# Re-set planner constants, array modes told apart and a lag behind a bank's copy, in a two-layer attention and MoE kernel on one core

## The chip, the core and the metric

The kernel runs on one core of a Trainium2 chip. The metric is device time in microseconds (us) for one execution, from the first to the last instruction with what lies around them; lower is better. The kernel before takes 907.85 us, the median of three runs (905.75 to 908.74).

## What is computed

Three stages follow each other. Attention has 4 batches, 8 heads, 576 tokens and 64 features per head; it is linear attention with random features:

```python
def phi(x):
    proj = np.einsum('bhsd,md->bhsm', x, omega)          # 128 features
    h = proj - np.sum(x * x, axis=-1, keepdims=True) / 2.0
    return np.exp(h - np.max(h, axis=-1, keepdims=True)) / np.sqrt(m)
num = phi(q) @ (phi(k).T @ v);  den = phi(q) @ sum_s phi(k) + 1e-06
x = (num / den)                                          # 2304 tokens x 512
x = leaky(x @ w_in) @ w_out                              # layer one, d_ff 2048
x = (h * clip(h + 3, 0, 6) / 6) @ w2_out,  h = x @ w2_in # layer two, d_ff 2048
```

All inputs are float32. The products of the two layers keep float32 accuracy by splitting every operand in a high and a low part of type fp32r and adding three matmuls (high by high, low by high, high by low).

## The kernel before

The 2304 tokens are cut into five groups (512, 256, 512, 512, 512). Layer one (`moe1`) takes the groups in turn: for each of 16 blocks of 128 hidden features it runs 12 matmuls of the first product (`Hblk`, by `mm3`, lines L478 to L480), an activation, a split into parts `g`, and 12 matmuls of the second product (`Oblk`). Attention of a later group (`K_unit`, `Q_unit`) is mixed between these products. Attention of the first group (`Q_first`) runs alone at the start, since nothing else is ready there.

TensorE's array is used in three ways. The layers' products and the transposes use all of it. The scores of attention (`scores` and `K_tail`, L721 and L742) use two halves of 64 rows; two products of attention (L790 in `K_unit`, L949 in `Q_unit`) use two halves of 64 columns.

Layer two (`moe2`) has a Strassen-like scheme for the groups of 512 tokens: seven products of half size in place of eight, both in the first product (`Hpair`, 7 products of 6 matmuls with 256 columns each, L1122) and in the second (`down`, 7 products of 3 matmuls, L1044). In `Hpair` four of the seven products (b11, t2, t3, t4) are accumulated one after another in the same half of one bank, R[0]. After b11, t2 and t3 ScalarE or VectorE copies this half to SBUF (`save`, a copy through the helper at L463 and L464), and the next product may write the half only when the copy is done; after t4 it is copied once more. The four adds between the quarters that `down` needs (`parts`, through `plus` and `add_alts`, L471 on VectorE, L472 on GpSimd) and the split in high and low parts (`halves`) run between `Hpair` and `down`.

No order is written by hand. Every step is an `Op` in a `Graph`: its alternatives (engine, cost in ns, function), a due time, the buffers that it takes and the steps that it depends on. `Graph.run` repeats one thing: among the steps whose inputs are planned, it takes the one that can start first by its own clocks (within 60 ns the one due first), picks the engine that ends it first (with a `BIAS` against VectorE, 300 ns in the last phase) and emits it. So each engine's order is fixed when the program is built. A step of attention on TensorE also waits in the plan for `SLACK` (2000 ns) after it is ready, or for `FOLLOW` (400 ns) if the step before it on TensorE was one of attention too, and a change between the two kinds is planned with `SWITCH` (110 ns). In the first stage planned gaps of TensorE are half filled with matmuls on zeros (`keep_warm`, L1317), 15 of them ahead of everything. Due times of layer two come from `UP` and `DOWN` (ns for one pair of blocks), `LAG_A` (how many pairs `down` stays behind), `READY`, `XLEAD` and `SOON`.

## Time and profile before

| what | value |
|---|---|
| median of three runs | 907.85 us (905.75 to 908.74) |
| the profiled execution | 907.79 us, of which the span from first to last instruction 906.0 us |
| TensorE busy (PE) | 892.0 us, 98% of the span |
| weight loads busy (PEld) | 796.2 us, 88% |
| VectorE (DVE), ScalarE (ACT), GpSimd (POOL) | 617.0, 492.8, 332.0 us |
| granted TensorE clock | 1.0 in all but the first and last instants |
| HBM traffic | 217 GB/s over the span |

The profile is one execution on the core. PE is TensorE's matmuls, PEld its weight loads, which run beside them. The end of a matmul is modelled (two follow each other much faster than one seems to last), so the pace of TensorE is read from start to start, or from how many matmuls lie in a stretch, and not from its busy share. By time there are three stages: attention of the first group alone (to about 49 us), layer one with the rest of attention (to about 536 us), and layer two.

### The profile page before, as it was taken

Reading aid. Unit: us, or ns where it says so; the run is one execution under the profiler, and the core shown is the slowest. Engines: PE = TensorE matmul, PEld = TensorE weight load, DVE = VectorE, ACT = ScalarE, POOL = GpSimd, SP = SyncE. Lnnn points to the kernel's source line nnn. Section 1 sums busy time; section 2 is a strip of 40 time slices with the busy share of each in tenths; the row PEclk is TensorE's granted clock in tenths of the full one; section 3 lists DMA queues with packets and bytes.
Section 4 is the critical chain, followed back from the end, with each engine's and each line's share of the span. In section 5 each row is a group of like instructions: output and inputs, shape, how many; then the busy total and the mean of one; then the engine's idle time right before and its main releaser. Section 6 shows DMA issues by size and latency. Waiting matters only on the chain.

```text
span 906.0 us, 17804 instructions
## 1 busy us (share of the span) xinstructions
PE 892.0 (98%) x6349; PEld 796.2 (88%) x6349; DVE 617.0 (68%) x1464; ACT 492.8 (54%) x1155; POOL 332.0 (37%) x559
## 2 busy tenths in 40 slices
PE   8999999999999999999999999999999999999998
PEld 8878888889777877888888888999999999999997
DVE  5998877877897976555687344675665658666554
ACT  6966674866776555544455345543443444445442
POOL 3454454544535321101010003244426436454642
PEclk9999999999999999999999999999999999999999
DMA  9556644677557555978899349885786684677540
GB/s 333 152 167 215 204 153 139 208 228 232 149 171 223 178 166 178 367 286 314 292 343 349 95 140 326 280 296 168 244 311 218 201 260 131 224 242 231 167 134 28
DMA packets 91497, 198.01 MB, mean 219 GB/s; under 512 B 14736, under 2 KB 40976, under 8 KB 91408
## 3 DMA queue, kind: packets, MB, share of 16 engines
q1 hardware_dynamic: 91408, 196.87, 65.7%
q8 instruction: 50, 0.82, 0.4%
q14 instruction: 39, 0.32, 0.1%
HBM read 150.18 MB, written 46.66 MB: 217 GB/s over the span
## 4 chain that ended last, share of the span: by engine, by line
PE 91%; DVE 4%; ACT 2%; issue 1%; DMA 1%; POOL 1%; SPq 0%; DVEq 0%; POOLq 0%; ACTq 0%
PE bank L1044 18%; PE bank L1122 17%; PE bank L478 15%; PE bank L480 15%; PE bank L479 15%; PE bank L721 4%; PE bank L768 1%; PE bank L949 1%; PE bank L918 1%; PE bank L790 1%; DVE junk L892 1%; PE bank L844 1%; DMA late_w<-in 1%; DVE nm L686 1%; PE bank L779 0%
## 5 line engine op out<-in xcount | busy, mean ns | idle before, releaser
L1044 PE MATMUL bank<-w,g 128*128 128x256 f32 x762 | 108.1, 279 | 0.4 <-DVE g L467 0.2
L1044 PEld LDWEIGHTS bank<-w,g 128*128 128x128 f32 x762 | 96.9, 188 | 1.0 <-DVE g L467 0.7
L464 ACT COPY late_u<-bank 128x256 f32<-128x256 f32 (+1 forms) x112 | 43.1, 386 | 95.1 <-PE bank L1122 86.4
L986 DVE TENSOR_TENSOR g<-bank,g 128x512 fp32r<-128x512 f32 (+1 forms) x80 | 50.8, 635 | 60.9 <-ACT g L464 60.2
L984 ACT ACTIVATE bank<-bank 128x512 f32<-128x512 f32 (+1 forms) x80 | 43.8, 548 | 76.2 <-PE bank L480 76.0
L1122 PE MATMUL bank<-x,late_w 128*128 128x256 f32 x552 | 74.0, 281 | 0.9 <-DVE u L1065 0.7
L697 ACT ACTIVATE h<-bank,nm 128x128 f32<-128x128 f32 x228 | 63.5, 390 | 18.9 <-POOL nm L692 18.7
L1122 PEld LDWEIGHTS bank<-x,late_w 128*128 128x128 f32 x552 | 68.2, 189 | 1.5 <-DVE u L1065 0.9
L1122 PE MATMUL bank<-second_w,late_w 128*128 128x256 f32 x498 | 68.5, 281 | 0.5 <-ACT late_u L464 0.5
L478 PE MATMUL bank<-g,w 128*128 128x512 f32 (+1 forms) x180 | 68.9, 383 | 0.0
L478 PE MATMUL bank<-x,w 128*128 128x512 f32 (+1 forms) x180 | 68.7, 382 | 0.1
L480 PE MATMUL bank<-g,w 128*128 128x512 f32 (+1 forms) x180 | 66.3, 368 | 0.8 <-DVE g L986 0.8
L480 PE MATMUL bank<-x,w 128*128 128x512 f32 (+1 forms) x180 | 66.4, 369 | 0.5 <-POOL x L468 0.5
L479 PE MATMUL bank<-g,w 128*128 128x512 f32 (+1 forms) x180 | 66.2, 368 | 0.0
L479 PE MATMUL bank<-x,w 128*128 128x512 f32 (+1 forms) x180 | 66.2, 368 | 0.0
L1122 PEld LDWEIGHTS bank<-second_w,late_w 128*128 128x128 f32 x498 | 62.4, 189 | 0.8 <-ACT late_u L464 0.7
L686 DVE TENSOR_REDUCE nm<-bank 128x4 f32<-128x512 f32 (+2 forms) x76 | 48.1, 654 | 15.8 <-PE bank L721 15.7
L1044 PE MATMUL bank<-second_w,g 128*128 128x256 f32 x333 | 48.8, 280 | 0.0
L903 POOL TENSOR_TENSOR h<-h,den 128x512 f32<-128x512 f32 (+2 forms) x32 | 33.1, 1038 | 41.8 <-DVE den L898 25.4
L692 POOL TENSOR_TENSOR nm<-nm,sq 128x4 f32<-128x4 f32 (+2 forms) x76 | 25.2, 344 | 60.2 <-DVE nm L689 57.2
L478 PE MATMUL bank<-x,second_w 128*128 128x512 f32 (+1 forms) x120 | 45.2, 377 | 0.3 <-ACT h L697 0.3
L472 POOL TENSOR_TENSOR xr<-late_xr 128x128 f32<-128x128 f32 x38 | 19.3, 526 | 70.7 <-DVE late_xr L1160 70.7
(361 smaller groups left out, 2449.9 us busy)
## 6 DMA issues: line engine op xcount, KB each, us to landing
late_w<-in SPq DMA_DIRECT2D x84, 512.0 KB, 4.5
in<-late_w SPq DMA_DIRECT2D x32, 512.0 KB, 3.8
late_w<-in SPq DMA_DIRECT2D x40, 256.0 KB, 4.5
third_w<-in SPq DMA_DIRECT2D x20, 512.0 KB, 4.4
wst<-w2i SPq DMA_DIRECT2D x16, 512.0 KB, 4.2
wst<-w2o SPq DMA_DIRECT2D x16, 512.0 KB, 4.1
x_t<-late_w SPq DMA_DIRECT2D x12, 512.0 KB, 4.5
wst<-w1i SPq DMA_DIRECT2D x10, 512.0 KB, 4.6
```

The lines of the kernel that those rows point to most:

```text
L464: return [("act", c_act(n, psum), lambda: nc.scalar.copy(dst(), src())), dve if psum else dve + (True,)]
L478: nc.tensor.matmul(o, lhsT=ah, rhs=bh, start=start, stop=False)
L479: nc.tensor.matmul(o, lhsT=al, rhs=bh, start=False, stop=False)
L480: nc.tensor.matmul(o, lhsT=ah, rhs=bl, start=False, stop=stop)
L686: g.op([("dve", c_dve(c * 128), lambda raw=raw, n_=n_: nc.vector.tensor_reduce(out=n_()[:, :, 0], in_=raw(), axis=AX.X, op=ALU.min))], rd= ...
L697: nc.scalar.activation(h.tiles[0][:, q * 128:q * 128 + 128], raw()[:, q], AF.Exp, bias=nm.tiles[0][:, q], scale=-1.0)
L721: nc.tensor.matmul(ps[bank].tiles[0][o, at:at + 128], lhsT=src.tiles[0][r, k * one + i * 128:k * one + i * 128 + n], rhs=wn[r], start=True ...
L903: eng.tensor_tensor(out=x, in0=x, in1=den.tiles[1][:, 0:c].to_broadcast([128, c, 128]), op=ALU.mult)
L984: g.op([("act", c_act(n, True), lambda: nc.scalar.activation(P(), P(), AF.Prelu, alpha=0.01))], wr=[p], due=d)
L986: g.op([("dve", c_dve(n), lambda: nc.vector.tensor_tensor(out=G1(), in0=P(), in1=G0().bitcast(F32), op=ALU.subtract))], rd=[p, (gg, 0)], w ...
L1044: nc.tensor.matmul(acc[bank].tiles[0][:, half * 256:half * 256 + 256], lhsT=src.tiles[x][:, q * 128:q * 128 + 128], rhs=w[k].tiles[y][:, c ...
L1122: nc.tensor.matmul(R[r](), lhsT=w[x], rhs=m[y], start=start and k == n == 0, stop=k == 1 and n == 2, skip_group_check=True)
```

## The change

The planner now tells modes of the array apart. Each attention step on TensorE has a mode: S (halves of rows), N (halves of columns) or F (the whole array); products of the layers are M. How long a step waits in the plan after it is ready depends on its mode and on that of the step before it; a turn from one mode to another has a planned cost of its own. In layer two a product into R[0] that accumulates on a half copied before (t2, t3, t4) is planned at least `APART` = 100 ns after it is ready, so that another ready step may go first. `LAT`, costs, caps on live buffers, due times and lags are re-set, the first stage gets a fourth buffer `xT`, and `BIAS2`, the planner's bias against VectorE in the last phase, falls from 300 to 200 ns. What is computed, the number of matmuls of the computation and their shapes stay as they are.

```diff
-SLACK = 2000.0
-FOLLOW, SWITCH = 400.0, 110.0
+SLACK = 1.0
+PACE = 2.215
+WAIT = {"S": 4000.0, "N": 1000.0, "F": 1500.0}
+FOLLOW = 400.0
+MATE = 400.0
+TURN = {("M", "S"): 193.0, ("M", "N"): 92.0, ("S", "M"): 205.0, ("N", "M"): 158.0, ("F", "S"): 193.0, ...
-NW1 = 10
+NW1 = 11
-BIAS2 = 300.0
+BIAS2 = 200.0
-ATT = [None, (32e3, 132e3), (132e3, 182e3), (182e3, 240e3), (240e3, 300e3)]
+ATT = [None, (32000.0, 132000.0), (132e3, 178000.0), (182e3, 236000.0), (240e3, 305000.0)]
-UP, DOWN = 7.2e3, 2.5e3
+UP, DOWN = 7100.0, 2600.0
+APART = 100.0
-LAG_A, XLEAD, SOON, READY = 3.0, 9e3, 10e3, 14e3
+LAG_A, XLEAD, SOON, READY = 2.5, 6000.0, 13000.0, 15000.0
...
-    LAT = 150.0
+    LAT = 165.0
-    CAP = {"x2": 5, "s": 2, "h": 4, "sum": 4, "raw": 6}
+    CAP = {"x2": 6, "s": 1, "h": 6, "sum": 4, "raw": 6}
...
-        last = False
+        last = "M"
...
-                at = o.ready + (FOLLOW if o.slack and last else o.slack) + o.lazy
+                at = o.ready + (self.wait(o.mode, last) if o.slack else 0.0) + o.lazy
...
-                if last != (o.slack > 0.0):
-                    clock["pe"] += SWITCH
-                    o.end += SWITCH
-                last = o.slack > 0.0
+                turn_ = TURN.get((last, o.mode), 0.0)
+                clock["pe"] += turn_
+                o.end += turn_
+                last = o.mode
...
+    @staticmethod
+    def wait(mode, last):
+        if mode == "F":
+            return FOLLOW if last != "M" else WAIT["F"]
+        return MATE if last in "SN" else FOLLOW if last == "F" else WAIT[mode]
...
-    first, more = room("first", [("h", 6, ([128, 512], F32)), ("xT", 3, ([128, 512], F32)), ("xn", 2, ([128, 8, D], F32)),
+    first, more = room("first", [("h", 6, ([128, 512], F32)), ("xT", 4, ([128, 512], F32)), ("xn", 2, ([128, 8, D], F32)),
...
-                g.op([("pe", 6 * c_mm(256), mm)], rd=[c[a], b], wr=[bank[r]], due=t0 + UP * at)
+                g.op([("pe", 6 * c_mm(256), mm)], rd=[c[a], b], wr=[bank[r]], due=t0 + UP * at, lag=APART if r == 0 and not start else 0.0)
```

What this does to the program shows in the order of the instructions. The lines named here are 13 higher in the changed kernel (L1122 becomes L1135, L1044 becomes L1057, L472 becomes L485); a row is one instruction, with the number of equal ones behind an x.

**TensorE in layer two**, the seventh pair of blocks of the third group, from t2 to t4. R[0] is in bank_177 before and in bank_178 in the changed kernel; rows of L1044 and L1057 are products of `down`. Before:

```order
L1122 MATMUL bank_177<-second_w_4_0_1024,third_w_0_0_1595 128x256 x6
L1044 MATMUL bank_176<-w_95,g_105 128x256 x3
L1044 MATMUL bank_180<-w_94,g_105 128x256 x3
L1122 MATMUL bank_177<-second_w_3_0_1023,late_w_2_0_3977 128x256 x6
L1044 MATMUL bank_179<-w_96,g_105 128x256 x3
L1044 MATMUL bank_175<-w_97,g_106 128x256 x3
L1122 MATMUL bank_177<-x_101,late_w_3_0_3978 128x256 x6
```

Now:

```order
L1135 MATMUL bank_178<-w_92,late_w_0_0_3974 128x256 x6
L1057 MATMUL bank_182<-second_w_0_0_1054,g_106 128x256 x3
L1057 MATMUL bank_176<-w_98,g_105 128x256 x3
L1057 MATMUL bank_181<-w_98,g_105 128x256 x3
L1057 MATMUL bank_176<-second_w_0_0_1054,g_105 128x256 x3
L1057 MATMUL bank_183<-w_99,g_105 128x256 x3
L1135 MATMUL bank_178<-second_w_3_0_1057,late_w_2_0_3976 128x256 x6
L1135 MATMUL bank_177<-x_103,late_w_3_0_3977 128x256 x6
L1135 MATMUL bank_180<-x_104,late_w_3_0_3977 128x256 x6
L1135 MATMUL bank_178<-x_101,third_w_0_0_1613 128x256 x6
```

Between one product into R[0] and the next there were 6 matmuls; now there are 15 and 12, partly of `down` and partly of the next pair.

**TensorE in the first stage**, from the second gap that is filled with matmuls on zeros. Before (the rows that follow are the product L768 of attention, which needs the features of the first K unit):

```order
L1317 MATMUL bank_182<-zero 128x384 x12
L768 MATMUL bank_180<-first_v_0_0_169,ht_0_152 128x132
L768 MATMUL bank_180<-first_v_0_0_169,first_h_0_0_158 128x66
L768 MATMUL bank_180<-first_v_0_0_169,first_h_1_0_159 128x66
L768 MATMUL bank_180<-first_v_0_0_169,first_h_0_0_158 128x66
```

Now (L734 is the scores, from the fourth buffer `first_xT_3`):

```order
L1330 MATMUL bank_183<-zero 128x384 x5
L734 MATMUL bank_181<-wn,first_xT_3_0_167 128x128
L734 MATMUL bank_182<-wn,first_xT_3_0_167 128x128
L734 MATMUL bank_181<-wn,first_xT_3_0_167 128x128
L734 MATMUL bank_182<-wn,first_xT_3_0_167 128x128
L734 MATMUL bank_181<-wn,first_xT_3_0_167 128x128
L734 MATMUL bank_182<-wn,first_xT_3_0_167 128x128
L734 MATMUL bank_181<-wn,first_xT_3_0_167 128x128
L734 MATMUL bank_182<-wn,first_xT_3_0_167 128x128
L1330 MATMUL bank_183<-zero 128x384 x4
L781 MATMUL bank_176<-first_v_0_0_170,ht_0_152 128x132
```

The scores of a third unit moved into the gap; in the whole stage 45 matmuls on zeros became 34.

**The adds of `parts`**, at the end of the third group of layer two. Before, on GpSimd, the four adds each for two sets of quarters (one set in xr_0_115, one in xr_0_112):

```order
L468 TENSOR_TENSOR second_w_1_0_1021<-xr_0_113,second_w_1_0_1021 128x512
L472 TENSOR_TENSOR xr_0_115<-late_xr_1_0_3986 128x128 x2
L472 TENSOR_TENSOR xr_0_115<-xr_0_115,late_xr_1_0_3986 128x128
L472 TENSOR_TENSOR xr_0_112<-wst_0_108 128x128
L472 TENSOR_TENSOR xr_0_115<-late_xr_1_0_3986,xr_0_115 128x128
L472 TENSOR_TENSOR xr_0_112<-xr_0_112,wst_0_108 128x128
L472 TENSOR_TENSOR xr_0_112<-wst_0_108 128x128
L472 TENSOR_TENSOR xr_0_112<-wst_0_108,xr_0_112 128x128
```

Now, on VectorE, behind its work on the last pair of the group:

```order
L1173 SCALAR_TENSOR_TENSOR late_xr_1_0_3985<-bank_180,late_u_0_0_3979 128x2x128
L1173 SCALAR_TENSOR_TENSOR wt_0_111<-bank_180,late_u_0_0_3979 128x2x128
L480 TENSOR_TENSOR g_105<-xr_0_114,g_105 128x512
L480 TENSOR_TENSOR g_107<-late_xr_1_0_3985,g_107 128x384
L484 TENSOR_TENSOR xr_0_113<-xr_0_113,late_xr_1_0_3985 128x128
L484 TENSOR_TENSOR xr_0_113<-late_xr_1_0_3985 128x128
L484 TENSOR_TENSOR xr_0_113<-late_xr_1_0_3985,xr_0_113 128x128
L484 TENSOR_TENSOR xr_0_112<-xr_0_112,wst_0_108 128x128
```

In the whole program 170 adds of 128 columns moved from GpSimd (288 before, 118 now) to VectorE (none before).

## Rows read from the trace of the kernel before

**Rows 1.** Windows: length, busy us (count) of PE, PEld, DVE, ACT, POOL, clock, DMA, GB/s.

```profile
0.00:49.30 49.30, 45.08 (x405) 41.09 (x405) 37.05 (x95) 39.51 (x113) 19.78 (x46) 1.00 0.73 248
49.30:536.00 486.70, 483.59 (x2874) 394.80 (x2873) 357.95 (x881) 287.90 (x705) 149.60 (x206) 1.00 0.65 217
536.00:560.50 24.50, 23.25 (x169) 21.32 (x168) 9.73 (x23) 11.45 (x24) 5.89 (x12) 1.00 0.86 295
560.50:760.00 199.50, 199.50 (x1712) 199.50 (x1711) 124.94 (x285) 91.98 (x188) 89.43 (x169) 1.00 0.74 245
769.00:868.50 99.50, 99.50 (x850) 99.50 (x849) 59.86 (x131) 45.58 (x96) 47.53 (x95) 1.00 0.67 210
```

**Rows 2.** Waits of PE in layer two (536 to 902 us): us, times, longest.

```profile
PE bank L1122 <- ACT late_u L464: 0.8, 3, 0.5
```

**Rows 3.** A window inside layer two, columns as in rows 1.

```profile
592.00:621.00 29.00, 29.00 (x259) 29.00 (x258) 18.39 (x41) 11.14 (x22) 14.28 (x29) 1.00 0.73 256
```

**Rows 4.** Timeline of PE from 703.9 us: start, length, what, count [idle before].

```profile
703.91 1.58 PE L1122 MATMUL bank<-x,late_w 128*128 128x256 f32 x12
705.33 1.58 PE L1044 MATMUL bank<-second_w,g 128*128 128x256 f32 x12
...
768.64 0.62 PE L1122 MATMUL bank<-x,late_w 128*128 128x256 f32 x3 [0.70 <-DVE u L1065]
```

**Rows 5.** Timeline of PE from 620.5 us: t3, the next product, t4.

```profile
620.54 0.84 PE L1122 MATMUL bank<-second_w,late_w 128*128 128x256 f32 x6
621.22 0.84 PE L1122 MATMUL bank<-x,late_w 128*128 128x256 f32 x6
621.90 0.92 PE L1122 MATMUL bank<-x,third_w 128*128 128x256 f32 x6
622.65 0.52 PE L1044 MATMUL bank<-w,g 128*128 128x256 f32 x3
```

**Rows 6.** Timeline of ACT, same place: the copy of R[0] after t3.

```profile
621.42 0.37 ACT L464 COPY late_u<-bank 128x256 f32<-128x256 f32 x1 [1.98 <-PE bank L1122]
```

**Rows 7.** Timeline of PEld, same place: weight loads of these products.

```profile
621.11 0.76 PEld L1122 LDWEIGHTS bank<-x,late_w 128*128 128x128 f32 x6
621.84 0.77 PEld L1122 LDWEIGHTS bank<-x,third_w 128*128 128x128 f32 x6
```

**Rows 8.** Timeline of PE in the first stage.

```profile
9.34 2.35 PE L1317 MATMUL bank<-zero 128*128 128x384 f32 x12
11.53 0.39 PE L768 MATMUL bank<-first_v,ht 128*128 128x132 f32 x2
...
40.48 0.65 PE L862 MATMUL bank<-ident,u 128*128 128x128 f32 x4 [1.18 <-DVE u L853]
```

**Rows 9.** Timeline of PE in layer one, around one use of half arrays.

```profile
51.97 0.39 PE L480 MATMUL bank<-x,w 128*128 128x512 f32 x1
52.28 1.09 PE L742 MATMUL bank<-wn,xT 64*64 64x128 f32 x16
53.30 0.50 PE L478 MATMUL bank<-x,w 128*128 128x512 f32 x1
53.65 0.40 PE L479 MATMUL bank<-x,w 128*128 128x512 f32 x1
```

**Rows 10.** Groups by line and form, 560 to 900 us: busy, mean ns | idle before.

```profile
L464 ACT CAST g<-xr 128x512 fp32r<-128x512 f32 x35 | 21.7, 620 | 22.5 <-POOL xr L472 11.8 <-PE bank L1044 9.6 <-POOL g L468 1.2
L467 DVE TENSOR_TENSOR g<-xr,g 128x512 fp32r<-128x512 f32 x46 | 33.3, 726 | 6.9 <-ACT g L464 6.7
L1155 ACT ACTIVATE bank<-late_u,point 128x512 f32<-128x512 f32 x40 | 27.6, 693 | 2.4 <-DVE late_u L1133 1.1
L472 POOL TENSOR_TENSOR xr<-late_xr 128x128 f32<-128x128 f32 x34 | 17.6, 534 | 42.0 <-DVE late_xr L1160 42.0
L1133 DVE TENSOR_TENSOR late_u<-late_u,bank 128x256 f32<-128x256 f32 x36 | 15.1, 420 | 35.9 <-PE bank L1122 18.9 <-ACT late_u L464 16.1 <-ACT x L464 0.8
L1160 DVE SCALAR_TENSOR_TENSOR late_xr<-bank,late_u 128x256 f32<-128x256 f32 x30 | 12.0, 415 | 0.1
```

More of the change, by code (lines that the diff above doesn't have):

```diff
@@ L40 @@
 ORDERLY = ("first",)
[L41 removed]
+NW1 = 11
 LEAD = 0.8
[L43 removed]
+BIAS2 = 200.0
 PAD = 48
[L45 to L50 removed]
+O1, O2 = 11000.0, 12000.0
+T0 = 42000.0
+L1 = [100000.0, 50000.0, 127000.0, 87e3, 87e3]
+ATT = [None, (32000.0, 132000.0), (132e3, 178000.0), (182e3, 236000.0), (240e3, 305000.0)]
+RAW = (150000.0, 302000.0)
+PREP = (330000.0, 400000.0)
 EARLYX = [0, 2, 3]
[L52 to L54 removed]
+UP, DOWN = 7100.0, 2600.0
+LAZY = 2000.0
+APART = 100.0
+LAG_A, XLEAD, SOON, READY = 2.5, 6000.0, 13000.0, 15000.0
 PARTS = [[(0, 4, False), (1, 0, True)], [(1, 1, True), (2, 3, False)], [(2, 1, False), (3, 3, True)], [(3, 0, True), (4, 4, False)]]
@@ L76 @@
 class Op:
-    __slots__ = ("alts", "due", "slack", "allocs", "bufs", "deps", "ndep", "out", "ready", "end", "eng", "seq", "phase", "second", "cost", "lazy")
+    __slots__ = ("alts", "due", "slack", "allocs", "bufs", "deps", "ndep", "out", "ready", "end", "eng", "seq", "phase", "second", "cost", "lazy", "mode")
 class Graph:
-    LAT = 150.0
+    LAT = 165.0
     MORE = {"dve": 80.0, "act": 90.0, "pool": 80.0}
@@ L100, in __init__, with op @@
         self.todo = {}
-    def op(self, alts, rd=(), wr=(), due=0.0, also=(), late=False):
+    def op(self, alts, rd=(), wr=(), due=0.0, also=(), late=False, lag=0.0, mode="F"):
         o = Op()
@@ L105, in op @@
         self.todo[o.phase] = self.todo.get(o.phase, 0) + 1
-        o.alts, o.due, o.seq, o.lazy = alts, due, len(self.ops), LAZY if late else 0.0
+        o.alts, o.due, o.seq, o.lazy = alts, due, len(self.ops), LAZY if late else lag
         o.slack = self.slack if alts[0][0] == "pe" else 0.0
+        o.mode = mode if o.slack else "M"
         o.out, o.ready, o.end, o.eng = [], 0.0, None, None
@@ L329, in c_mm @@
 def c_mm(n):
[L330 removed]
+    return 114.0 if n == 256 else max(112.0, n / PACE)
 def c_dma(nbytes):
@@ L722, in mm @@
                                          rhs=wn[r], start=True, stop=True)
-        g.op([("pe", nh * (f + half) * 228.0, mm)], rd=[src], wr=ps, also=hs, due=due)
+        g.op([("pe", nh * (f + half) * 224.0, mm)], rd=[src], wr=ps, also=hs, due=due, mode="S")
         features(ps, hs, cols, before, sq, due, nh)
@@ L743, in mm @@
                                      start=True, stop=True)
-        g.op([("pe", HP * 228.0, mm)], rd=[src], wr=[p], also=[h], due=due)
+        g.op([("pe", HP * 224.0, mm)], rd=[src], wr=[p], also=[h], due=due, mode="S")
         features([p], [h], [HP], [0], sq, due)
@@ L791, in kvt @@
                                      start=i == 0, stop=i == 4)
-        g.op([("pe", 5 * 224.0, kvt)], rd=hs + [ht, v], wr=[p], also=[zr, kf], due=due + 3e3)
+        g.op([("pe", 5 * 224.0, kvt)], rd=hs + [ht, v], wr=[p], also=[zr, kf], due=due + 3e3, mode="N")
         mid = lambda: kf.tiles[0].rearrange("p h c -> p (h c)")[:, 0:128]
@@ L950, in num @@
                                      rhs=tq.tiles[0][:, e, k * n:k * n + n], start=True, stop=True)
-        g.op([("pe", max(230.0, N * 1.92), num)], rd=[tq] + kf, wr=[p], also=[x for x, _ in outs], due=due + 6e3)
+        g.op([("pe", max(214.0, N * 1.88), num)], rd=[tq] + kf, wr=[p], also=[x for x, _ in outs], due=due + 6e3, mode="N")
         for k, (hp, (xr, at)) in enumerate(zip(hps, outs)):
@@ L1243, in weights @@
                 Buf.NOW = 1 if i < NW1 else 2 if i < 2 * FT - 3 * ST2 // 2 else 0
-                d.append(weight(src, j, SG[0] + step * (j + o) - 4e3))
+                d.append(weight(src, j, SG[0] + step * (j + o) - 4000.0))
         Buf.NOW = 0
```

9 lines of the change are left out of this document (2 added, 7 removed).

## The prediction

> **What bounds the kernel now.** I read the windows by stage first. After the first stage TensorE (PE) is the only engine that is nearly always at work: in layer one it is idle for 486.70 - 483.59 = 3.1 us, in most of layer two for nothing, while VectorE (DVE) is busy 63% of the longest stretch there and ScalarE and GpSimd under half [rows 1]. The amount of matmul work is not changed. So only four things can move the time: what TensorE does for nothing (fillers, turns of the array's mode), where it waits, how early layer one can start, and the pace at which its matmuls follow each other. The waits are few: the list of them in layer two has 0.8 us for ScalarE's copies at three places, all of them where the two layers meet [rows 2].
>
> The pace is the surprise. A busy share of 100% hides it; one has to count. In the stretch from 592 to 621 us 259 matmuls are listed, some three of which began before it, so 256 in 29.0 us: 0.1133 us each [rows 3]. Twelve matmuls of the same kind from 703.91 on take (705.33 - 703.91)/12 = 0.118 us each [rows 4]. TensorE runs in either of two paces, about 4.5 ns apart, for long stretches, at the same granted clock of 1.00.
>
> What switches it shows at 621.9 us. Each product there is six matmuls: 620.54 to 621.22 and 621.22 to 621.90 are 0.68 us each, but the third takes 0.75 us (621.90 to 622.65) [rows 5]. It is t4, which writes the bank half R[0] that ScalarE copied after t3. With six matmuls in between, the copy runs from 621.42 to 621.79 [rows 6]; the product's weight load starts at 621.84, only 0.06 us ahead of its matmul, where the load before it had 0.11 us [rows 7]. The copy ends some 0.05 us too late. The product loses that, and from there TensorE stays in the slower pace. I followed this through the timeline of layer two. Of the 96 products that write a half copied before, 44 have at most six matmuls between. From 565.0 to 829.6 us there are 39 such, and all show a stumble of 25 to 53 ns; of the 52 with nine matmuls or more none shows it (one waits longer for another reason). After 560 us the pace went from fast to slow 13 times, each time at a stumble, and came back at 11 stumbles and two longer waits. Without an event it never changed.
>
> **The change, part by part.** The sum goes against the profiled execution (907.79 us; span 906.0), which stands at the median of 907.85.
>
> *Products behind the copy.* In the changed order only six of the 96 have at most six matmuls between, five of them in the first 170 matmuls of layer two, the sixth some 2170 matmuls in, of 3080. What slow pace and stumbles cost now: in 199.5 us stand some 1710 matmuls, which at 0.1133 us are 193.7 us; in the 99.5 us from 769 on some 848, or 96.1 us [rows 1, 3]. That is 5.8 + 3.4 = 9.2 us. Left in the changed kernel: the sixth short gap should drop TensorE into the slow pace until a wait frees it. The next place where the order has a product close behind a copy is 640 matmuls on: 640 x 4.5 ns = 2.9 us (bounds: 0 if something frees it at once, 4.1 us if nothing does to the end). So -6.3 us. The work that now fills the gaps is products of `down` or of the next pair that had to be done anyway; the cost is nothing as long as their operands are there (third rival).
>
> *Modes told apart.* Between a product and scores in half rows the start-to-start time is 0.31 us (51.97 to 52.28) against 0.23 us between products, and the first product behind takes 0.35 us (53.30 to 53.65): some 0.1 us a turn [rows 9]. I counted turns into, out of and between the half-array modes in both orders, from the first product of layer one on: 94 before, 93 now. So -0.1 us: the grouping hardly groups. The Trainium skill, TensorEngine Tiling (Array Packing), on mode switching, says that a change of tiling mode drains TensorE; by it the grouping would be the part that pays, and by the count of the order it pays for one drain.
>
> *First stage.* 45 matmuls on zeros become 34. Twelve of them take 11.53 - 9.34 = 2.19 us, so 0.18 us each, and 11 are 2.0 us [rows 8]. They fill gaps in which nothing was ready, so they pay only if real work takes their place; the order shows that it does (the scores of a third unit in the gap at 9.34). Bounds: 0 if the gaps stay and are merely empty; -3.2 us if the wait of 1.2 us for VectorE at 40.48 goes too [rows 8]. The transpose that waits there has more work ahead of it in the new order, but a product of attention elsewhere follows its copy more closely. I take -2.0. Layer one then begins so much earlier, and since TensorE is busy to within 3.1 us of all of it, that arrives at the end.
>
> *Rest of layer one.* The order is another one throughout. The 3.1 us of idle time could go, or as much again could come [rows 1]; I take 0.
>
> *Lags, caps, due times; the meeting of the layers.* TensorE is idle there for 24.50 - 23.25 = 1.25 us now [rows 1]. The new order has two copies followed by three matmuls less, and products of `down` behind a copy by three matmuls at three places for one; 0, between -1.25 and +1.25.
>
> *Adds from GpSimd to VectorE.* 170 adds of 0.53 us leave GpSimd [rows 10]; on VectorE each costs at most the 0.42 us of twice the columns, so VectorE gets up to 71 us in some 365 us, from 63% towards 82% [rows 1, 10]. It stays off the path unless `down` waits (third rival). 0.
>
> Sum: -6.3 - 0.1 - 2.0 = -8.4, so 907.8 - 8.4 = **899.4 us**.
>
> **The rivals.**
>
> *The slow pace stays (slower).* TensorE came back to the fast pace mostly at stumbles. If it enters the steady part of layer two slow and there are no stumbles left, nothing frees it: some 2900 matmuls x 4.5 ns = 13.0 us in place of 9.2, so +3.8. With turns and the first stage 907.8 + 3.8 - 2.1 = 909.5; with nothing won at the start 911.5. It is decided at the product with no matmul behind its copy, at matmul 165 of layer two: does TensorE leave that wait fast? Against it: of nine waits of about 0.1 us or more in layer two eight were followed by the fast pace; the ninth, which ended at 768.64, was not [rows 4].
>
> *No headroom in layer two.* Weight loads are busy for 199.50 of 199.50 us there, and for 29.00 of 29.00 in the fast stretch too [rows 1, 3]. If the load path sets the pace and the two paces have another cause than the copies, the 9.2 us stay but for the stumbles (39 x some 0.035 = 1.4 us): 907.8 - 1.4 - 2.1 = 904.3; if those come elsewhere, 905.7. The Trainium skill, Perfetto Trace Analysis, section Identifying the Most-Contended Engine, has weight-load busy share as the good measure of TensorE's headroom; by it layer two has none and the time would be that. The trace disagrees in so far as both paces show 100%.
>
> *`down` waits at the ends of groups.* The new order runs the first products of a group's last pair 37 matmuls (37 x 0.1133 = 4.2 us) behind its last product of `Hpair`, where it was 61; their path by rows is 0.42 + 0.69 + 2 x 0.42 + 0.62 + 0.73 = 3.3 us [rows 10]. The next ones come 61 matmuls behind (6.9 us), with four adds of at most 0.53 us, a second copy and a subtraction more: 3.3 + 2.1 + 1.35 = 6.8 us. It just fits, if VectorE takes them at once. If each of the eight places is late by 0.8 us, 899.4 + 6.4 = 905.8.
>
> **How the numbers follow.** Forecast 0.72; no headroom 0.10; `down` waits 0.10; slow pace stays 0.05; disturbed start or layer one 0.03. Range: the best case is 9.2 + 3.2 + 0.1 with some of layer one's idle time, 894.5; upwards it takes in the second and third rival, to 906.5. A measurement here tells 0.3% or 2.7 us from no change: 905.1 to 910.6. The forecast and the lower parts of the two middle rivals lie below: faster 0.80, same 0.13, slower 0.07.
>
> **What would show it.** Right: in layer two windows at 0.1133 us a matmul nearly throughout, six-matmul rows of L1135 at 0.84 us, weight loads 0.11 us ahead, with a slow part from about matmul 2170 of layer two on; the first L491 near 47.3 us where L478 began at 49.3; the idle time of layer one about as now. Wrong: long stretches at 0.118 us with no stumble at their start, or a list of waits in which L1057 waits for DVE `g`, or a first stage that still ends at 49 us with waits in place of fillers.

## The result, and the profile after

The changed kernel takes 897.17 us (median of 8 executions, 895.98 to 903.37) beside 907.35 us for the kernel before (8 executions, 904.17 to 908.74) on the same chip; the ratio is 0.9906, with a 95% interval of 0.9879 to 0.9932. That is faster by more than 0.3%, and 2.2 us below the forecast of 899.4. Two more sets of the same kernel gave 0.9909 (0.9893 to 0.9924) and 0.9908 (0.9889 to 0.9928).

The profiled execution took 903.37 us, with a span of 901.2: it is the slowest of the eight, 6 us above the median, and much of what follows is about why. The busy line of its page, to set beside the table of before:

```profile
PE 889.7 (99%) x6338; PEld 795.3 (88%) x6338; DVE 660.7 (73%) x1663; ACT 480.5 (53%) x1127; POOL 243.7 (27%) x388
```

The adds went from GpSimd (332.0 to 243.7 us) to VectorE (617.0 to 660.7 us). The windows by stage answer to [rows 1]; four further ones inside layer two answer to [rows 3] (same columns):

```profile
0.00:45.45 45.45, 42.27 (x394) 38.93 (x394) 36.32 (x96) 36.68 (x108) 16.06 (x44) 1.00 0.74 258
45.45:527.74 482.29, 480.92 (x2863) 393.64 (x2861) 362.95 (x890) 280.36 (x689) 157.25 (x212) 1.00 0.66 218
...
556.00:626.00 70.00, 70.00 (x597) 70.00 (x596) 51.22 (x133) 31.58 (x63) 12.96 (x26) 1.00 0.73 248
630.00:702.00 72.00, 72.00 (x638) 72.00 (x636) 52.70 (x140) 31.11 (x63) 13.04 (x27) 1.00 0.76 258
725.00:783.00 58.00, 58.00 (x495) 58.00 (x494) 45.94 (x117) 27.25 (x55) 14.39 (x23) 1.00 0.56 184
796.00:861.00 65.00, 65.00 (x555) 65.00 (x554) 43.59 (x115) 29.60 (x61) 11.44 (x22) 1.00 0.63 201
```

Layer one begins at 45.45 us instead of 49.33, layer two at 527.74 instead of 536.03. Of the second gain 12 matmuls of layer one, 0.227 us each, are only moved behind that point (1500 of 512 columns lie ahead of it, 1512 before), 2.7 us. So the first stage gave 3.9 us and layer one 536.03 - 49.33 - (527.74 - 45.45) - 2.7 = 1.7 us. Layer two, from there to the last product, is 896.96 - 527.74 - 2.7 = 366.5 us, where it was 901.71 - 536.03 = 365.7: **in the profiled execution layer two, which was to give 6.3 us, gave nothing.**

The windows show where it went. Three matmuls in each list began before it: 594 in 70.0 us are 0.1178 us each, 635 in 72.0 us 0.1134, 492 in 58.0 us 0.1179, 552 in 65.0 us 0.1178. TensorE is in the slow pace in three of the four windows, at the same granted clock. Its timeline shows where the slow stretches begin (start, length, what, count [idle before]):

```profile
550.91 0.94 PE L1057 MATMUL bank<-w,g 128*128 128x256 f32 x6 [0.93 <-ACT bank L1168]
551.69 0.87 PE L1135 MATMUL bank<-w,late_w 128*128 128x256 f32 x6
...
554.59 1.68 PE L1135 MATMUL bank<-w,late_w 128*128 128x256 f32 x12 [0.60 <-DMA late_w<-in]
...
722.79 2.48 PE L1135 MATMUL bank<-x,late_w 128*128 128x256 f32 x19 [0.16 <-DMA late_w<-in]
```

In this trace the long ones shown begin behind waits, not behind stumbles: the one of 0.60 us at 554.59 for a DMA leaves TensorE slow for 615 matmuls, the one of 0.16 us at 722.79 for the next 524. The list of waits of TensorE in layer two (from 546 us on) is short, as that of before was:

```profile
PE bank L1057 <- ACT bank L1168: 0.9, 1, 0.9
PE bank L1135 <- DMA late_w<-in: 0.8, 2, 0.6
PE bank L1135 <- ACT u L477: 0.5, 1, 0.5
PE bank L1057 <- DVE g L480: 0.2, 1, 0.2
```

To go on I counted the intervals from the start of one matmul of 256 columns to the next in layer two, in each trace. "Slow" are matmuls of `Hpair` and `down` with an interval of 117 to 126 ns, and the pace is what intervals up to 126 ns have above 113.3 ns; "stumbles" is what intervals from 126 to 180 ns have above it, "waits" what longer ones have.

| layer two in the trace of | slow matmuls of some 2850 | pace, us | stumbles, us | waits, us |
|---|---|---|---|---|
| before | 1739 | 8.0 | 1.5 | 4.7 |
| changed | 1946 | 8.8 | 0.1 | 5.7 |
| changed, 2nd and 3rd trace (below) | 1952, 1735 | 8.8, 7.9 | 0.1, 0.0 | 4.9, 6.2 |
| before with the lag alone | 1560 | 7.1 | 0.3 | 6.0 |
| changed without the lag | 1663 | 7.6 | 0.8 | 7.8 |
| changed, adds on GpSimd | 293 | 1.5 | 0.2 | 9.3 |
| changed, one mode | 1273 | 5.8 | 0.1 | 4.9 |
| changed, 32 cuts and 8 cuts | 151, 465 | 1.0, 2.3 | 1.8, 0.5 (cuts included) | 6.6, 4.8 |

The count of slow matmuls leaves out the group of 256 tokens, whose 192 matmuls of this width add 0.9 us of slow pace in the three traces of the changed kernel, 0.4 in before, with the lag alone and with one mode, and nothing in the other rows. With them in, what is left of layer two without pace, stumbles and waits is 353.8 us in all three traces of the changed kernel, without the lag, with the adds on GpSimd and with one mode, and 351.0 in before and with the lag alone, which is the same less the 2.7 us of the 12 matmuls. So in these traces layer two differs by pace, stumbles and waits and by nothing else.

### The profile page after: what moved, and what is told of

It is laid out like the page before. It is cut to its first block, busy times and chain, and to the rows that moved or that the text cites. A ratio compares the mean times of both kernels' runs of the same rounds, so it can differ in the third digit from the quotient of the medians.

```text
span 901.2 us, 17816 instructions
## 1 busy us (share of the span) xinstructions
PE 889.7 (99%) x6338; PEld 795.3 (88%) x6338; DVE 660.7 (73%) x1663; ACT 480.5 (53%) x1127; POOL 243.7 (27%) x388
## 4 chain that ended last, share of the span: by engine, by line
PE 90%; DVE 4%; DMA 3%; ACT 1%; POOL 1%; issue 1%; SPq 0%; DVEq 0%; POOLq 0%; ACTq 0%
PE bank L1057 19%; PE bank L1135 17%; PE bank L491 15%; PE bank L493 14%; PE bank L492 14%; PE bank L734 4%; PE bank L781 2%; DMA late_w<-in 1%; PE bank L962 1%; PE bank L931 1%; PE bank L803 1%; DVE junk L905 1%; DVE nm L699 1%; DMA out_raw<-wt 1%; PE bank L857 1%; DMA first_xT<-kT 1%
## 5 line engine op out<-in xcount | busy, mean ns | idle before, releaser
L477 ACT COPY late_u<-bank 128x256 f32<-128x256 f32 (+1 forms) x98 | 37.7, 385 | 116.1 <-PE bank L1135 97.1
L1057 PE MATMUL bank<-w,g 128*128 128x256 f32 x633 | 89.0, 280 | 1.4 <-ACT bank L1168 0.9
L1057 PEld LDWEIGHTS bank<-w,g 128*128 128x128 f32 x633 | 80.3, 189 | 2.4 <-ACT bank L1168 1.1
L1135 PE MATMUL bank<-x,late_w 128*128 128x256 f32 x576 | 75.1, 280 | 0.2 <-DMA late_w<-in 0.2
L1135 PEld LDWEIGHTS bank<-x,late_w 128*128 128x128 f32 x576 | 70.5, 189 | 0.6 <-DVE xr L484 0.3
L1057 PE MATMUL bank<-second_w,g 128*128 128x256 f32 x387 | 56.1, 280 | 0.0
L1135 PE MATMUL bank<-w,late_w 128*128 128x256 f32 x384 | 52.8, 280 | 0.6 <-DMA late_w<-in 0.6
L1057 PEld LDWEIGHTS bank<-second_w,g 128*128 128x128 f32 x387 | 50.1, 189 | 0.0
L1135 PEld LDWEIGHTS bank<-w,late_w 128*128 128x128 f32 x384 | 48.5, 189 | 1.1 <-DMA late_w<-in 0.8
L905 DVE CUSTOM_DVE_ANT_0 junk<-h,zr 128x128 bf16<-128x128 f32 (+1 forms) x128 | 46.0, 398 | 1.3 <-ACT zr L477 0.3
```

What stands on the lines that cost most here:

```text
L477: return [("act", c_act(n, psum), lambda: nc.scalar.copy(dst(), src())), dve if psum else dve + (True,)]
L905: nc.vector.tensor_tensor_reduce(out=jk.tiles[0][r, q % 2], in0=h.tiles[0][r, q * 128:q * 128 + 128], in1=zr[k].tiles[0][r, e], scale=1.0, ...
L1057: nc.tensor.matmul(acc[bank].tiles[0][:, half * 256:half * 256 + 256], lhsT=src.tiles[x][:, q * 128:q * 128 + 128], rhs=w[k].tiles[y][:, c ...
L1135: nc.tensor.matmul(R[r](), lhsT=w[x], rhs=m[y], start=start and k == n == 0, stop=k == 1 and n == 2, skip_group_check=True)
```

## The experiments

Four sets of runs were made, each with the kernel before beside it on the same chip. The kernel before took 906.98, 906.07, 900.59 and 906.29 us in them (medians of 24, 23, 17 and 11 executions); so a time is read against its own set alone.

**The changed kernel again** (first set, no edit).

> The changed kernel once more, unchanged. Theory A (TensorE keeps one of two paces in layer two, 0.1133 or 0.1178 us a matmul; without stumbles only a wait can change it, and which pace a wait leaves is not the same in every execution): its times spread again over some 895 to 904 us, and the new profile's span differs from the 901.2 us of the first one by 4.5 ns for each matmul more or less at the slow pace (1946 then), to within 1 us; layer one begins at 45.4 +- 0.3 and layer two at 527.7 +- 0.7 us as before. Rival B (the executions differ in loads of the first stage and the waits of layer one): the difference of the spans lies ahead of 527.7 us, and layer two takes 369.2 +- 1 us again.

899.1 us, 897.41 to 902.32, ratio 0.9909 (0.9893 to 0.9924). The profiled execution took 902.32, again the slowest. It begins layer one at 45.71 and layer two at 527.51, and from there it reads like the first trace: 1952 slow matmuls. So the stages ahead of layer two repeat, as theory A has it. But layer two takes 368.4 us, which is within rival B's 369.2 +- 1 as well, so this run does not decide between them. Both traces are of slow executions; what the faster ones do in layer two isn't in a trace. They are up to 7 us shorter, and the profile has 8.8 us of slow pace for that, so this theory has room for them; that is argued, not shown.

**The lag alone**, in the kernel before.

```diff
+APART = 100.0
...
-        ... o.lazy = alts, due, len(self.ops), LAZY if late else 0.0
+        ... o.lazy = alts, due, len(self.ops), LAZY if late else lag
...
-                g.op([("pe", 6 * c_mm(256), mm)], ..., due=t0 + UP * at)
+                g.op([("pe", 6 * c_mm(256), mm)], ..., due=t0 + UP * at, lag=APART if r == 0 and not start else 0.0)
```

> The kernel before with only the lag of 100 ns behind the copy of R[0] (5 of 96 such products are left with at most six matmuls in between, 44 before; stage one and layer one keep their order). Prediction's term: -6.3 us, 901.0. Theory A: stumbles gone for certain (-1.4 us), the slow pace gone in part by chance, so 898 to 906 with a spread of several us and a profile whose slow matmuls explain its place. Rival C (the lag gives nothing, the gain of the change sits in stage one and layer one): 906 to 908.

905.29 us, ratio 0.9984 (0.9974 to 0.9994): 1.5 us, about what the stumbles are worth. Short gaps are products into R[0] with at most six matmuls between them and the product whose half was copied. With 5 of them in place of 44 TensorE still spent 1560 matmuls in the slow pace. Most of these go back to one of the five, the product at 638.78 us (lines are 1 higher than in the kernel before):

```profile
638.78 0.92 PE L1123 MATMUL bank<-second_w,late_w 128*128 128x256 f32 x6
639.54 1.22 PE L1045 MATMUL bank<-w,g 128*128 128x256 f32 x9
640.60 0.64 PE L1123 MATMUL bank<-x,late_w 128*128 128x256 f32 x4
```

Its six matmuls take 0.76 us, and the next nine 0.118 us each. TensorE stays slow, through one wait and one further stumble, until 760.5 us: some 1020 of the 1560 slow matmuls, 4.6 us. This is the mechanism of the prediction, at a gap that the lag did not remove. The list of waits in layer two shows what else the new order brought:

```profile
PE bank L1045 <- DVE g L468: 1.5, 3, 1.0
PE bank L1123 <- ACT late_u L465: 1.4, 3, 0.5
PE bank L1045 <- DVE late_u L1066: 0.2, 1, 0.2
```

`down` now waits 1.5 us for `g`, where the list of before has 0.2:

```profile
PE bank L1044 <- DVE g L467: 0.2, 1, 0.2
```

My -6.3 is refuted for the lag by itself.

**The changed kernel without the lag** (`APART = 0.0`).

> The changed kernel with the lag set to 0 (25 of 96 products into R[0] with at most six matmuls in between, 6 with the lag). Theory A: some 20 stumbles of 25 to 53 ns (0.7 us) return, each of those that hits the fast pace drops TensorE to the slow one: 899 to 904 us, less spread from one execution to the next than the changed kernel shows. Rival C: 897 +- 1.

903.96 us, ratio 0.9970 (0.9958 to 0.9983), against 0.9909 in the same set: there the lag is worth 899.1 to 904.0, some 5 us. In the timeline the stumble is back (start to start 0.76 us for six matmuls at 620.25), and the next ones are slow (0.71 us for six at 621.36):

```profile
620.25 0.92 PE L1135 MATMUL bank<-x,late_w 128*128 128x256 f32 x6
621.01 0.52 PE L1057 MATMUL bank<-third_w,g 128*128 128x256 f32 x3
621.36 0.87 PE L1057 MATMUL bank<-second_w,g 128*128 128x256 f32 x6
622.07 0.52 PE L1057 MATMUL bank<-third_w,g 128*128 128x256 f32 x3
```

So the same lag gives 1.5 us in the one kernel and 5 in the other: it needs something that the rest of the change supplies. The 5 us are in the times alone. The trace without the lag is of an execution near its median (903.65 us), and its span of 901.7 is only 1.5 us above that of the slowest execution with the lag in this set: it has more waits (7.8 against 4.9 us) and stumbles (0.8 against 0.1), but less slow pace.

**The first stage's part**, in the kernel before: a fourth buffer `xT`, and `NW1 = 11`.

> The kernel before with a fourth buffer xT in the first stage and NW1 11 (41 matmuls on zeros, 45 before, 34 in the changed kernel); layer two keeps its order. If the fourth buffer makes the earlier start of layer one (49.3 to 45.4 us), the first product begins at 45.5 to 47.5 us and the time falls by 2 to 3.9 us, to 903.5 to 905.4. If the start comes from the re-set lags, due times and waits of the planner, it begins at 48.6 to 49.3 us and the time is 906.7 to 907.5.

In the profile the buffer does what it was to do: layer one begins at 46.94 us, layer two at 534.07 instead of 536.03, and layer two, in the unchanged order, is as long as before (365.7 us). The profiled execution took 906.12, but the median is 907.35 and the ratio 1.0001 (0.9991 to 1.0011). The 2 us are in the trace and not in the times. The executions of either kernel differ by over 3 us; which part of them takes the 2 us back isn't known.

**Stage one and layer one of the change with the old numbers of layer two** (`APART = 0.0`, and before's `UP, DOWN`, `LAG_A, XLEAD, SOON, READY` and `BIAS2`).

> The changed kernel with lag 0 and before's UP, DOWN, LAG_A, XLEAD, SOON, READY and BIAS2: stage one and layer one of the changed kernel (34 matmuls on zeros), a layer two close to that of before (45 short gaps, 44 before; 299 adds on GpSimd, 297 before). If the profiles' earlier start of layer two (536.0 to 527.7 us, 2.7 us of it matmuls moved behind that point) is worth the same in every execution, 5.6 us stay: 901.4 +- 1. If stage one and layer one are worth nothing at the median (as the run with the fourth buffer hints), 906 to 907.

908.14 us, ratio 1.0013 (0.9999 to 1.0027). Layer two begins at 530.19 us, 5.8 earlier, and is 369.2 us long, 3.5 more. Its waits (from 527 us on) are 8.9 us by the count, 4.7 before; the longest groups:

```profile
PE bank L1057 <- DVE g L480: 2.2, 4, 1.0
PE bank L1135 <- ACT u L477: 1.0, 2, 0.9
PE bank L1057 <- DVE late_u L1078: 0.5, 2, 0.3
```

An earlier start that layer two's planning does not follow is given back as waits there, 4.2 of 5.8 us in the profile. The rest did not arrive at the median either. Which of the old numbers makes the waits was not tested.

**The adds back on GpSimd** (`BIAS2 = 300.0` in the changed kernel; same lag, 6 short gaps).

> The changed kernel with BIAS2 300 in place of 200: 299 adds on GpSimd and 69 on VectorE (129 and 239 in the changed kernel), same lag, still 6 short gaps. My prediction had the adds at 0: 898 +- 1. Theory D (the lag pays only because the adds went to the faster VectorE; with them on GpSimd products of the second half wait for their operands, as the run with the lag alone shows with 6.0 us of stalls): 901 to 904, with more and longer waits of L1057 for DVE g.

904.94 us, 899.25 to 907.15, ratio 0.9973 (0.9956 to 0.9991), so some 5 us of the gain are gone (899.63 us in the same set for the run with one mode, below, whose layer two is that of the changed kernel): my 0 for the adds was wrong. The profiled execution is the fastest of its 12, with only 293 slow matmuls, and in spite of that its span is 897.5, since waits take 9.3 us. From 527 us on:

```profile
PE bank L1135 <- DMA late_w<-in: 1.3, 3, 0.7
PE bank L1057 <- DVE g L480: 1.2, 3, 0.5
PE bank L1057 <- ACT bank L1168: 0.9, 1, 0.9
PE bank L1135 <- ACT u L477: 0.5, 1, 0.5
PE bank L1135 <- ACT late_u L477: 0.5, 1, 0.5
PE bank L1057 <- DVE u L1078: 0.3, 1, 0.3
```

Products of `down` wait for `g` (1.2 us, 0.2 in the changed kernel). This is the mechanism of theory D, and the trace shows a part of it. What an execution at the median spends, 5.7 us more than this one, isn't in a trace; and the planner also put TensorE's products of layer two in another order here, so the adds are not the only difference. One group of the adds tells their price: twelve take 601 ns each on GpSimd here, twelve 284 ns on VectorE in the changed kernel (groups by line and form, 560 to 896 us); over all adds of this shape in the two programs it is 533 and 301 ns. GpSimd's:

```profile
L485 POOL TENSOR_TENSOR late_xr<-late_xr,xr 128x128 f32<-128x128 f32 x12 | 7.2, 601 | 0.2
```

VectorE's, in the changed kernel:

```profile
L484 DVE TENSOR_TENSOR late_xr<-late_xr,xr 128x128 f32<-128x128 f32 x12 | 3.4, 284 | 0.0
```

**One mode for all of attention**, in the changed kernel:

```diff
-        if mode == "F":
-            return FOLLOW if last != "M" else WAIT["F"]
-        return MATE if last in "SN" else FOLLOW if last == "F" else WAIT[mode]
+        return FOLLOW if last != "M" else 2000.0
...
-                turn_ = TURN.get((last, o.mode), 0.0)
+                turn_ = 110.0 if (last == "M") != (o.mode == "M") else 0.0
```

> The changed kernel with before's rule for attention on TensorE (wait 2000 ns, or 400 behind attention, and 110 ns for each change between the two kinds, no modes): layer two in the identical order, stage one with the same 34 zeros, 111 changes of mode in place of 109. My term for the modes was -0.1 us: the same as the changed kernel to within 0.7 us. Theory A: its profile, one more execution of the same layer two, shows another sequence of slow and fast stretches or the same one as the two before (slow from 554 to 627 and from 722 on).

899.63 us (896.16 to 903.12), ratio 0.9920 (0.9891 to 0.9949): the median can't tell it from the changed kernel. The profile can, ahead of layer two:

```profile
0.00:46.41 46.41, 43.32 (x394) 39.83 (x394) 36.24 (x95) 36.65 (x107) 16.16 (x44) 1.00 0.74 253
46.41:529.63 483.22, 480.91 (x2863) 394.00 (x2862) 362.45 (x888) 282.34 (x693) 160.13 (x212) 1.00 0.65 217
```

Layer one takes 483.22 us; in the three traces of the changed kernel it is 481.8 to 482.3. So by one trace of it the rule on modes is worth 0.9 to 1.4 us there, where I had 0.1. (Layer two begins at 529.63 instead of 527.5 to 528.0; the rest of that lies in stage one, which ends anywhere from 45.4 to 46.6 us in the traces with this first stage.) TensorE's busy time is the same, 480.91 us here and 480.92 in the first trace of the changed kernel; what differs is idle time, 2.3 us here and 1.2 to 1.4 in the changed kernel. The longest wait is one that the changed kernel doesn't have:

```profile
PE bank L732 <- ACT h L708: 1.1, 1, 1.1
```

I had counted turns of the mode, and neither their number nor their price makes the difference. From a product to scores it takes 318 ns from start to start at the median of 28 turns here and 319 ns at that of 26 in the changed kernel (318 in the kernel before), from scores to column halves 202 ns in all three. Of these turns only the ones that hold a wait are much longer, one of 1442 and one of 787 ns here. The order of layer two is the same to the last matmul, and its trace has another course of paces: 1273 slow matmuls. So an identical order does run with different shares of the slow pace. Half of the slow matmuls here come from the sixth short gap, the product at 786.26 us, matmul 2166 of layer two:

```profile
785.58 0.84 PE L1133 MATMUL bank<-x,late_w 128*128 128x256 f32 x6
786.26 0.92 PE L1133 MATMUL bank<-second_w,late_w 128*128 128x256 f32 x6
787.02 0.87 PE L1133 MATMUL bank<-x,late_w 128*128 128x256 f32 x6
```

The six matmuls ahead of it take 0.68 us, its own six 0.76, and TensorE stays slow until 861.83 us, for some 639 matmuls with one more stumble among them.

**A cut in every pair.** One matmul of t3 is cut in two of 128 columns, in the changed kernel:

```diff
+                            if a == 2 and k == 1 and n == 1:
+                                for e in range(2):
+                                    nc.tensor.matmul(R[r]()[:, e * 128:e * 128 + 128], lhsT=w[x], rhs=m[y][:, e * 128:e * 128 + 128],
+                                                     start=False, stop=False, skip_group_check=True)
+                                continue
```

> The changed kernel with one matmul of t3 in each of 32 pairs of blocks cut in two of 128 columns (32 matmuls more). Each cut is one short disturbance of the same form. By itself some 0.11 us each, 3.5 us in all. Theory A1 (what pace follows a disturbance hangs on its form): the pace behind the cuts is nearly always the same; always fast would give back up to 8.8 us of the profile's slow pace, always slow would hold all of layer two at 0.1178 (+13 - 8.8 us). Theory A2 (chance): both paces follow, in some 10 to 22 of the 32 places each. Rival (the pace has nothing to do with disturbances): stretches change at other places than cuts and waits.

898.95 us (896.94 to 900.08), ratio 0.9911 (0.9890 to 0.9933). 151 slow matmuls are left. A cut as the timeline of TensorE has it:

```profile
567.24 0.62 PE L1140 MATMUL bank<-second_w,late_w 128*128 128x256 f32 x4
567.69 0.33 PE L1137 MATMUL bank<-second_w,late_w 128*128 128x128 f32 x2
567.86 0.33 PE L1140 MATMUL bank<-second_w,late_w 128*128 128x256 f32 x1
568.03 1.20 PE L1140 MATMUL bank<-w,late_w 128*128 128x256 f32 x9
```

The two halves take 0.17 us and the matmul behind them 0.17 us, and some three more are a little late; in all a cut costs 127 ns (median of the 32), so the 32 cost 4.1 us. Where neither products of 512 columns nor a wait follow at once the pace behind a cut is the fast one each time. That is theory A1, the pace hangs on the form of the disturbance, or else a cut only keeps a fast pace that was there, since nearly all of these cuts met it. By the ratios (0.9911 and 0.9909) 32 cuts gain nothing over the changed kernel.

**Cuts in two pairs of each group** (the same with `and i in (1, 5)`), third set.

> The changed kernel with the cut of one matmul of t3 in pairs 1 and 5 of each group only (8 cuts, 126 ns each by the run with 32, so +1.0 us; order otherwise that of the changed kernel). Theory A1 (behind a cut the pace is the fast one, whatever it was): slow stretches end at the next cut, the profile shows at most some 700 slow matmuls (3 us) where the first two profiles had 1946 and 1952; the median 895 to 897.5 us and the spread of the executions smaller than the 7 us of the changed kernel. Theory A2 (a cut only keeps a fast pace that was there): slow stretches run through cuts, 898 to 900.

896.30 us (894.12 to 898.25), ratio 0.9947 (0.9932 to 0.9962) against a kernel before that took only 900.59 there. The profile decides between the theories. Windows ahead of and behind the two cuts that met the slow pace, at 575.76 and 806.16 us (columns as above):

```profile
555.00:575.00 20.00, 20.00 (x172) 20.00 (x171) 13.41 (x36) 9.43 (x20) 2.60 (x6) 1.00 0.90 298
577.00:625.00 48.00, 48.00 (x426) 48.00 (x425) 38.56 (x100) 21.71 (x44) 9.87 (x19) 1.00 0.68 238
786.00:805.00 19.00, 19.00 (x164) 19.00 (x163) 12.53 (x34) 10.00 (x21) 3.57 (x6) 1.00 0.86 287
808.00:857.00 49.00, 49.00 (x435) 49.00 (x434) 34.52 (x92) 23.28 (x47) 10.17 (x19) 1.00 0.61 193
```

With three matmuls taken off each, 0.1183 us becomes 0.1135, and 0.1180 becomes 0.1134. The timeline at the first of them:

```profile
575.29 0.63 PE L1140 MATMUL bank<-second_w,third_w 128*128 128x256 f32 x4
575.76 0.33 PE L1137 MATMUL bank<-second_w,third_w 128*128 128x128 f32 x2
575.93 0.34 PE L1140 MATMUL bank<-second_w,third_w 128*128 128x256 f32 x1
576.10 1.54 PE L1140 MATMUL bank<-w,late_w 128*128 128x256 f32 x12
```

That is theory A1: in both places a cut took TensorE out of the slow pace. 465 slow matmuls are left (2.3 us) for 1.0 us of cuts; the span of 895.0 is 4 to 6 us below those of the four traces of this order without cuts, which are from other chips. The kernel beats the one before by 4.3 us in this set. Whether it beats the changed one was not measured on one chip.

**The lag alone, with the 8 cuts**, same set.

> The kernel before with the lag alone and the same 8 cuts. The lag alone gave -1.5 us where the prediction had -6.3. If the rest is there but hidden by the slow pace that waits leave (1560 slow matmuls, 7.1 us, in its profile), the cuts bring some 5 of these 7.1 us for 1.0 us: 905.3 - 4 = 901.3 +- 1.5 us. If it went into waits or elsewhere, 906.3.

902.27 us: inside the range that I gave, but the kernel before took 900.59 beside it, and the ratio is 1.0020 (1.0012 to 1.0029). The time settles nothing for the other chips. The trace does in part: 417 slow matmuls instead of 1560, layer two 360.4 us instead of 364.9, 6.2 us of waits as without the cuts. So the pace was there to be had behind the lag; on this chip the kernel before seems to have had it already (no trace of it there).

**A lag of 200 ns, with the 8 cuts**, same set (`APART = 200.0`).

> The changed kernel with a lag of 200 ns (no short gap behind the first 170 matmuls of layer two; 6 with 100 ns have one) and the 8 cuts. Theory A1: as with the cuts alone, less one stumble and what slow pace follows it: 894.5 to 897.5 us. Against it: the order of the second half of layer two is another one, a new wait of some 0.5 to 1 us can take that back.

897.82 us, ratio 0.9966 (0.9954 to 0.9978), 0.3 us outside my range and 1.5 us above the cuts with 100 ns, which the intervals don't tell apart. In the trace 211 slow matmuls instead of 465 gain 1.1 us: the stumble at the sixth short gap is gone. The other order has 7.0 us of waits instead of 4.8.

**The changed kernel a third time**, fourth set.

> The changed kernel once more. The kernel before took 907.0, 906.1 and 900.6 us (medians) in the three sets of runs; the changed one has been set beside it only where it took 907. Theory A (what pace waits and stumbles leave decides 0 to 13 us of layer two in either kernel, and is drawn anew by chip and execution): beside a kernel before of 906 to 907 us the ratio is 0.990 to 0.992 again; beside one of some 900.6 us, which must then run layer two nearly all fast, the changed kernel takes 893.5 to 898 us, the gain of stage one, layer one and the stumbles alone (5.6 + 1.4 us at most). The profile's layer two less its slow pace, waits and stumbles is 353.8 us, as in the three profiles of this order so far. Rival (the chip or the memory makes other stages slower or faster, too): the boundaries of the stages (45.5 and 527.6 us) lie elsewhere by over 1 us.

899.22 us (896.34 to 903.18) beside 906.29, ratio 0.9908 (0.9889 to 0.9928). The profiled execution took 903.18, the slowest once more: 1735 slow matmuls, 6.2 us of waits, and 353.8 us for the rest of layer two, as in the first two. Layer one begins at 46.24, layer two at 528.02 us, so the stages keep their places to within 0.8 us in the three traces. It is theory A's first case; the set beside a kernel before of 900.6 us didn't come up, so what the change is worth on such a chip was not measured.

## Why the prediction was right, and where not

The total came out (899.4 forecast, 897.2 to 899.2 in three sets), the sum did not: by the traces the first stage and layer one gave 3.2 to 3.7 us more than forecast, and by the times layer two some 3 us less. That the two errors cancel is luck. By its steps:

- **Products behind the copy, -6.3.** The first half of the step holds: short gaps fell from 44 to 6, and the stumbles went. The mechanism mostly holds too: a product that comes too close behind its copy at the fast pace starts a slow stretch, as the one at 638.78 us did with the lag alone (interval 166 ns). Not every one does: with the lag and the 8 cuts the same product, at 639.06 us, has an interval of 162 ns and the fast pace goes on. The sixth short gap, matmul 2166 of layer two, does what was forecast where TensorE meets it at the fast pace. The trace with one mode, whose layer two has the order of the changed kernel, shows it at 786.26 us: slow for some 639 matmuls, 2.9 us, the term of the sum. (With the 8 cuts the same product, at 784.09, starts a slow stretch that lasts until the cut at 806.16.) In the three traces of the changed kernel this gap cost nothing: in the first and third TensorE was slow already, in the second a wait of 0.27 us for a DMA, one product ahead, let the copy end at 785.76 us, well ahead of the product at 786.39. What failed is the step that only such gaps matter: that TensorE "enters" steady layer two fast and stays so until matmul 2170. I had it from eight of nine waits in the trace of before. In the changed order the wait of 0.93 us for ScalarE at 550.91 left the slow pace in all three traces of it. The wait at matmul 165, where the prediction wanted it decided, left the slow pace in the second; in the other two a wait for a DMA followed six matmuls on and left the slow pace in one and the fast one in the other. And a disturbance at 714 to 722 us (not the same one each time) brought the slow pace back in each. The rival "the slow pace stays", at 0.05, describes the profiled executions. In the times, the lag is worth 5 us in the changed kernel and 1.5 in the one before.
- **Adds at 0.** Wrong: with the adds on GpSimd the gain is 0.27% instead of 0.9%. I had asked only whether VectorE has room for them, not whether `down` in the new order still has time for GpSimd's 0.46 to 0.6 us an add. That the lag, which pulls products of `down` forward, is what takes this time away is argued from the order, not shown by itself. The rival "`down` waits" had the right mechanism, but on the engine that the adds had left.
- **First stage, -2.0.** Measured -3.9, -3.6 and -3.1. Matmuls on zeros gave 1.8 us, as I had it; the listed waits of TensorE, 3.0 us without the one at the very start, fell to 2.0; the rest, some 1 us of busy time, I have not traced to a step. The lower bound of -3.2 had only one of these waits in it.
- **Modes, -0.1, and the rest of layer one, 0.** Together -1.7 to -2.2. The prediction's -0.1 for turns stands: there are 165 of all kinds in layer one with the rule and 169 without, at the same price. The error was the 0 for the idle time of layer one: it fell from 3.1 us [rows 1] to 1.4 (482.29 - 480.92) in the first trace and 1.2 in the other two, and the run with one mode puts 0.9 to 1.4 us of the gain on the rule, through waits. By the rule cited from the Trainium skill (TensorEngine Tiling (Array Packing), section Key Properties: a change of tiling mode drains TensorE) grouping should pay through fewer turns. The trace agrees that a turn costs something, 318 ns from a product to scores where the product takes 227, but no run here shows a gain by fewer turns.
- **No headroom (0.10).** The premise is refuted: weight loads are busy for all of 48.00 us in a fast window behind a cut and all of 20.00 us in the slow one ahead of it, and the pace changed there by 4.8 ns. The Trainium skill, Perfetto Trace Analysis, section Identifying the Most-Contended Engine, names that share, beside the achieved share of peak arithmetic, as the measure of TensorE's headroom; in these windows it is the same on both sides of a gain of 4%. The rival's other half, that the two paces have causes besides the copies, came true: waits changed the pace as well.

How the gain (8.2 to 8.5 us by the three ratios) divides is left open in one point. If the places of the stages in the traces hold in all executions, 5.3 to 5.8 us come ahead of layer two and some 3 in it. For the first part speak the other traces with these two stages (no lag, adds on GpSimd, 8 and 32 cuts, a lag of 200 ns), some of them of the fastest and middle executions: layer two begins at 527.3 to 528.9 us in all of them, and at 535.6 to 535.7 with the lag alone and the lag with cuts. The second part is in no trace of the changed kernel. But the run with the fourth buffer and the one with old numbers in layer two had earlier stages in the trace too, 2.0 and 5.8 us, and no gain in the median. What is shown is that neither the earlier start nor the lag gives its part alone.

## What to carry to other kernels

Where a product has to follow a copy closely, planning it a little later was worth it here only as far as the work pulled ahead found its operands, and one close follower left over can keep the loss: count those that remain, and give the chain of the work pulled ahead the faster engine in the same change. Before a gain is put on cheaper turns or steps, take the waits out of their mean, or look at the median. Where a matmul-bound stretch shows 100%, count matmuls per microsecond, ask what disturbance it entered with, and judge parts of a change by the places of stages in several traces and by times of one set, not by one profile. An engine that can stay in a slower pace makes an edit worth what its last disturbance leaves behind; a cheap one of a known form, placed behind the waits, is worth trying.

## What the runs showed of the hardware that was not expected

- The pace of 0.1133 or 0.118 us for matmuls of 256 columns is a state at the granted clock of 1.00. It outlasted products of other banks, tiles and lines for up to some 670 matmuls and changed only behind a disturbance, the smallest a single interval of 125 ns (second trace of the changed kernel, 783.47 us). From 560 us on, 44 intervals of 166 or 167 ns in these traces met the fast pace, and all 44 left the slow one.
- One matmul cut in two of 128 columns costs 127 ns and, where no wait or product of 512 columns follows at once, leaves the fast pace, also where the slow one was before (0.1183 to 0.1135 us at 575.76, 0.1180 to 0.1134 us at 806.16).
- The same kernel, the one before, took 906 to 907 us beside the changed one and in three sets of experiments, and 900.6 us in the third set, the only one on that chip. There is no trace of it there, so why is open.
- In three sets of three the profiled execution of the changed kernel was the slowest of its set. Why is open; in the other runs it stood anywhere from the fastest to the second slowest.
